# Converting double-precision weights on other engines, and keeping an activation in PSUM, in a convolution and MLP kernel

## The chip, the cores and the metric

The kernel runs on one core of a Trainium2 chip. The metric is the device time of one execution in microseconds (us). The core has five engines that run side by side and meet at semaphores: TensorE (PE in the profile, with its weight loads as PEld), VectorE (DVE), ScalarE (ACT), GpSimd (POOL) and SyncE (SP). SBUF is the working memory; PSUM holds the matmul results in eight banks.

## The reference

A sequence is filtered in the frequency domain, and the result goes through a two-layer MLP:

```python
X = np.fft.rfft(x, axis=1)                      # x: 8 x 3008 x 256, fp32
y = np.fft.irfft(X * (filt_r + 1j * filt_i), n=3008, axis=1).astype(np.float32)
h = y.reshape(24064, 256) @ w_in                # 256 x 2048
g = h * (1.0 / (1.0 + np.exp(-1.702 * h)))
out = (g @ w_out).astype(np.float32)            # 2048 x 256
```

[...]

## The kernel before, in words

Every fp32 product of the main part is made of three matmuls on a number split in two: a value rounded to the matmul type (suffix `h`, or `hi`) and the rest (suffix `l`, or `lo`); rounded by rounded, rounded by rest, rest by rounded.

The work has three parts. `first_fft` filters the first batch entry; its DMA-heavy part takes about the first 57 us. `weights` converts 16 units of weights (each 128 partitions x 512), interleaved with the end of `first_fft` and with the first MLP tiles. Then 48 MLP tiles of up to 512 tokens follow, 16 steps (`fc`) each, and the filtering of the next batch entry (`fft`, `signal`) is spread between the steps of the present one; the last batch entry's steps, from about 2150 us on, have nothing beside them.

One unit of weights (`weight`, lines 213 to 240): the upper and the lower 32 bits of each 64-bit number lie side by side as `top` and `low`. ACT takes |top| into `t` (L222); DVE clamps it (L227), shifts the exponent into place in `u` (L228), takes the bare exponent back into `t` (L229) and scales the low bits by it (L230); POOL adds the two (L231); ACT takes the absolute value (L232); DVE puts the sign back (L233). Then ACT rounds (`hi`, L238) and POOL takes the rest (`lo`, L239). The scratch tiles are the tile `w_tu` of the profile.

One MLP step (`mlp`, lines 526 to 566): `first(fc)` issues six matmuls (L539) into `ps`, a PSUM bank of tag `h`, of which there are two (`ps_h`, bufs=2). ACT reads the bank twice with the same activation: into `g` in SBUF as fp32 (L543), and into `gh` rounded (L544). DVE makes `gl = g - gh` (L545). `second(fc)` issues six matmuls (L555): four with `gh`, two with `gl`. `g`, `gh` and `gl` have two buffers each. The program text has `first(n+1)` ahead of `second(n)`.

The order of the instructions on each engine isn't that of the text: the framework's planner (`schedule_with_timeline_sim=True`) plays the program through with a model of the times and fixes an order for each engine; semaphores are set from the data that each instruction reads and writes. On the chip an engine takes its instructions in that fixed order. A PSUM bank may be written again when all its readers are done.

Of the kernel before, what the change touches and what calls it, by code (L numbers as in the profile page):

```python
# [9 lines left out]
F32 = mybir.dt.float32  # L10
F32R = mybir.dt.float32r
I64 = mybir.dt.int64
U32 = mybir.dt.uint32
AF = mybir.ActivationFunctionType
ALU = mybir.AluOpType
# [5 lines left out]
P = 128  # L21
# [4 lines left out]
LEAST = 2.0**-15  # L26
MOST = float(np.uint32(0x47EFFFFF).view(np.float32))
# [123 lines left out]
def tile_kernel(  # L151
# [9 lines left out]
    nc = tc.nc  # L161
    const = ctx.enter_context(tc.tile_pool(name="const", bufs=1))
    sb = ctx.enter_context(tc.tile_pool(name="sb", bufs=2))
# [49 lines left out]
    def weight(w, tu):  # L213

        if w.dtype != F32:
            rv = w.bitcast(U32).rearrange("p a (n k) -> p a n k", k=2)
            low, top = rv[:, :, :, 0], rv[:, :, :, 1]
            t, u = (a.bitcast(U32) for a in tu)
            w = t.bitcast(F32)


            ins = nc.scalar.activation(t.bitcast(F32), top.bitcast(F32), AF.Abs)  # L222
            if first[0]:
                tc.keep_in_program_order(ins)
                first[0] -= 1
            hi, lo = yield
            nc.vector.tensor_scalar(t.bitcast(F32), t.bitcast(F32), LEAST, MOST, ALU.max, ALU.min)  # L227
            nc.vector.tensor_scalar(u, t, 3, 0x40000000, ALU.logical_shift_left, ALU.bitwise_xor)  # L228
            nc.vector.tensor_scalar(t, u, 0xFF800000, None, ALU.bitwise_and)  # L229
            nc.vector.scalar_tensor_tensor(w, low, 2.0**-52, t.bitcast(F32), ALU.mult, ALU.mult)  # L230
            nc.gpsimd.tensor_tensor(w, u.bitcast(F32), w, ALU.add)  # L231
            nc.scalar.activation(w, w, AF.Abs)  # L232
            nc.vector.scalar_tensor_tensor(  # L233
                w.bitcast(U32), top, 0x80000000, w.bitcast(U32), ALU.bitwise_and, ALU.bitwise_or
            )
        else:
            hi, lo = yield
        nc.scalar.copy(hi, w)  # L238
        nc.gpsimd.tensor_tensor(lo, w, hi.bitcast(F32), ALU.subtract)  # L239
        yield  # L240

    def weights():

        todo, tus = [], None
        for i in range(NFC + 4):
            if i < NFC:
                todo.append(load_weight((w_out if i % 2 else w_in)[i // 2], f"w_{i}"))
            if i >= 4:
                if tus is None:
                    tus = const.tile([P, 4, 2, 2, D], F32, tag="zy", name="w_tu")  # L250
                for k in range(4 if i == 4 else 1):
                    k = k if i == 4 else i - 1
                    if k < NFC:
                        todo[k] = weight(todo[k], [tus[:, k % 4, m] for m in range(2)])
                        next(todo[k])
                n, o = divmod(i - 4, HALF)
                if n == len(wi_sb):
                    wi_sb.append(const.tile([P, 2, 2, DFF // 2], F32R, tag=f"wi_{n}", name=f"wi_{n}"))
                    wo_sb.append(const.tile([P, HALF, 2, D], F32R, tag=f"wo_{n}", name=f"wo_{n}"))
                if i % 2:  # L260
                    to = [wo_sb[n][:, o - 1 : o + 1, k] for k in range(2)]
                else:
                    to = [wi_sb[n][:, k, :, P * o : P * o + 2 * P] for k in range(2)]
                todo[i - 4].send(to)
            yield
# [260 lines left out]
    def mlp(b, t, y, nb, sums=(ps_o, "o")):  # L526

        w = P * nb
        pos, gs = [], {}

        def first(fc):
            ps = ps_h.tile([P, 512], F32, tag="h", name=f"h_{b}_{t}_{fc}")
            half, o = divmod(fc, HALF)
            c = slice(P * o, P * o + P)
            for n, (kc, wk, yk) in enumerate([(k, *q) for k in range(2) for q in ((0, 0), (0, 1), (1, 0))]):
                nc.tensor.matmul(ps[:, :w], wi_sb[half][:, wk, kc, c], y[:, yk, kc, :w], start=n == 0, stop=n == 5)  # L539
            g = sb.tile([P, 512], F32, tag="g", name=f"g_{b}_{t}_{fc}")  # L540
            gh = sb.tile([P, 512], F32R, tag="gh", name=f"gh_{b}_{t}_{fc}")
            gl = sb.tile([P, 512], F32R, tag="gl", name=f"gl_{b}_{t}_{fc}")
            nc.scalar.activation(g[:, :w], ps[:, :w], AF.Gelu_apprx_sigmoid)  # L543
            nc.scalar.activation(gh[:, :w], ps[:, :w], AF.Gelu_apprx_sigmoid)  # L544
            nc.vector.tensor_tensor(gl[:, :w], g[:, :w], gh[:, :w].bitcast(F32), ALU.subtract)  # L545
            gs[fc] = gh, gl

        def second(fc):
            if fc == 0:
                pos.extend(sums[0].tile([P, 512], F32, tag=sums[1], name=f"o_{b}_{t}_{m}") for m in range(2))  # L550
            gp = gs.pop(fc)
            wo = wo_sb[fc // HALF][:, fc % HALF]
            order = [(n, wk, gk, m) for n, (wk, gk) in enumerate(((0, 0), (1, 0), (0, 1))) for m in range(2)]
            for n, wk, gk, m in sorted(order, key=lambda q: q[3]) if fc == NFC - 1 else order:
                nc.tensor.matmul(  # L555
                    pos[m][:, :w], wo[:, wk, P * m : P * m + P], gp[gk][:, :w],
                    start=fc == 0 and n == 0, stop=fc == NFC - 1 and n == 2,
                )
            if fc == NFC - 1:
                o = sb.tile([P, 2, 512], F32, tag="out", name=f"out_{b}_{t}")  # L560
                nc.scalar.copy(o[:, 0, :w], pos[0][:, :w])
                nc.vector.tensor_copy(o[:, 1, :w], pos[1][:, :w])
                stores.append((out[:, :, done_w[0] : done_w[0] + w], o[:, :, :w]))
                done_w[0] += w

        return first, second

    def store():
# [40 lines left out]
    for n, (i, fc) in enumerate(turns):  # L609
        b, t = tiles[i]  # L610
# [61 lines left out]
```

## Time and profile before

| what | value |
|---|---|
| median of 3 runs | 2452.71 us (2450.07 to 2453.28) |
| time of the profiled execution | 2452.6 us |
| span of its instructions | 2450.6 us (2.0 us lie around it) |
| PE, DVE, ACT, POOL busy | 98%, 62%, 54%, 34% of the span |
| PE busy in the first 160 us | 125 us |
| PE idle after 160 us | 22 us |

The profile is one execution. A timeline row has a start, a duration, the engine, the line, the operation, what it writes and reads, and in square brackets the idle time of the engine before it with what ended it; a row may merge several instructions (xN). The other views group such rows.

### The profile page before, as it was taken

How to read it: one execution, taken by the hardware profiler on the slowest of the kernel's cores; microseconds unless marked ns; L12 is line 12 of the kernel's file. 1: busy time of each engine (PE TensorE's matmuls, PEld its weight loads, DVE VectorE, ACT ScalarE, POOL GpSimd, SP SyncE). 2: the span in 40 equal slices, each digit the busy share in tenths (PEclk: the TensorE clock that was granted, in tenths of full speed). 3: DMA queues.
4: the chain of work that ended last, by engine and by line, in shares of the span. 5: the costliest groups of instructions: out<-in, count | busy, mean ns of one | idle time of the engine just before them, and what ended most of it. 6: DMA issues, size and time to landing. Idle time of an engine off the chain costs nothing.

```text
span 2450.6 us, 31734 instructions
## 1 busy us (share of the span) xinstructions
PE 2394.2 (98%) x11082; PEld 1984.9 (81%) x11082; DVE 1531.4 (62%) x2167; ACT 1312.9 (54%) x2441; POOL 833.9 (34%) x714
## 2 busy tenths in 40 slices
PE   7799999999999999999999999999999999999999
PEld 6578888877888888888888887988888888898887
DVE  6966885488638883578636786368743777422322
ACT  5555655556555555555555565555555555444443
POOL 4743552265324441344323442234421444000000
PEclk9899999999999999999999999999999999999999
DMA  9234444545354435534344343444335443200000
GB/s 291 87 105 104 109 105 127 128 111 125 104 148 102 105 85 139 126 94 104 95 136 101 95 116 85 130 112 110 87 103 134 98 106 83 67 16 9 18 9 18
DMA packets 140927, 246.60 MB, mean 101 GB/s; under 512 B 15584, under 2 KB 81248, under 8 KB 140768
## 3 DMA queue, kind: packets, MB, share of 16 engines
q1 hardware_dynamic: 62528, 133.72, 19.4%
q10 hardware_dynamic: 53152, 66.80, 10.1%
q0 software_dynamic: 25088, 44.05, 9.3%
q8 instruction: 88, 1.44, 0.3%
q14 instruction: 71, 0.58, 0.1%
HBM read 150.67 MB, written 93.85 MB: 100 GB/s over the span
## 4 chain that ended last, share of the span: by engine, by line
PE 57%; DMA 2%; ACT 1%; issue 0%; ACTq 0%; SPq 0%; DVE 0%; POOLq 0%
PE o L555 26%; PE h L539 25%; PE i L512 2%; PE s L445 1%; PE i L445 1%; DMA b_d<-b 1%; DMA br<-b_d 1%; PE s L274 0%; PE s L273 0%; PE s L272 0%; DMA zy<-a_d 0%; DMA a_d<-al 0%; DMA x<-in_x_dram 0%; ACTq L419 0%; ACT g L543 0%
## 5 line engine op out<-in xcount | busy, mean ns | idle before, releaser
L539 PE MATMUL h<-y,wi 128*128 128x512 f32 (+1 forms) x4608 | 1172.5, 386 | 1.0 <-ACT y L520 1.0
L545 DVE TENSOR_TENSOR gl<-g,gh 128x512 fp32r<-128x512 f32 (+1 forms) x768 | 645.6, 843 | 751.9 <-ACT gh L544 677.6
L539 PEld LDWEIGHTS h<-y,wi 128*128 128x128 f32 x4608 | 861.9, 188 | 171.4 <-ACT y L520 1.4
L543 ACT ACTIVATE g<-h 128x512 f32<-128x512 f32 (+1 forms) x768 | 452.5, 589 | 909.6 <-PE h L539 767.1
L555 PE MATMUL o<-gh,wo 128*128 128x512 f32 (+1 forms) x3072 | 828.5, 389 | 6.6 <-ACT gh L544 6.1
L555 PEld LDWEIGHTS o<-gh,wo 128*128 128x128 f32 x3072 | 570.4, 188 | 125.0 <-ACT gh L544 11.4
L555 PE MATMUL o<-gl,wo 128*128 128x512 f32 (+1 forms) x1536 | 478.4, 388 | 14.3 <-DVE gl L545 14.1
L544 ACT ACTIVATE gh<-h 128x512 fp32r<-128x512 f32 (+1 forms) x768 | 448.9, 585 | 50.6 <-PE o L555 45.0
L460 POOL TENSOR_TENSOR zy<-c_buf,zy 48x512 fp32r<-48x512 f32 x224 | 335.3, 1497 | 93.6 <-DVE zy L459 83.6
L555 PEld LDWEIGHTS o<-gl,wo 128*128 128x128 f32 x1536 | 285.0, 188 | 76.2 <-DVE gl L545 22.2
L389 POOL TENSOR_TENSOR c_buf<-c_buf,u_buf 112x512 f32<-112x512 f32 x128 | 195.7, 1529 | 434.7 <-DVE c_buf L388 431.8
L409 POOL TENSOR_TENSOR xl<-x,xh 128x512 fp32r<-128x512 f32 x84 | 112.3, 1349 | 422.8 <-ACT xh L408 404.7
L428 POOL DMA_DIRECT2D zy<-a_d x224 | 128.3, 575 | 284.3 <-PE s L445 110.0
L396 DVE TENSOR_TENSOR c_buf<-s,c_buf 48x512 f32<-48x512 f32 x224 | 154.3, 689 | 14.9 <-ACT c_buf L395 8.6
L396 DVE TENSOR_TENSOR b<-i,b 48x512 f32<-48x512 f32 x224 | 154.1, 688 | 9.9 <-ACT b L395 3.8
L395 ACT COPY b<-i 48x512 f32<-48x512 f32 x224 | 130.1, 581 | 16.1 <-PE i L445 10.9
L395 ACT COPY c_buf<-s 48x512 f32<-48x512 f32 x224 | 130.2, 581 | 14.8 <-PE s L445 7.1
L459 DVE CAST zy<-c_buf 48x512 fp32r<-48x512 f32 x224 | 96.4, 430 | 52.2 <-POOL c_buf L389 48.5
L512 PEld LDWEIGHTS i<-tab,br 128*128 128x128 f32 x736 | 100.5, 194 | 19.1 <-issue 6.3
L512 PE MATMUL i<-tab,br 128*128 128x128 f32 x736 | 102.8, 279 | 7.8 <-DMA br<-b_d 4.4
L387 DVE TENSOR_TENSOR u_buf<-c_buf,f_buf 48x512 f32<-48x512 f32 x112 | 92.0, 821 | 3.6
L523 POOL CAST y<-carry 128x128 fp32r<-128x128 f32 x8 | 2.8, 377 | 262.4 <-PE h L539 262.3
(88 smaller groups left out, 1258.9 us busy)
## 6 DMA issues: line engine op xcount, KB each, us to landing
f_buf<-fs SPq DMA_DIRECT2D x224, 192.0 KB, 3.2
zy<-a_d POOLq DMA_DIRECT2D x224, 192.0 KB, 3.5
x<-in_x_dram SPq DMA_DIRECT2D x48, 512.0 KB, 4.8
out_dram<-out SPq DMA_DIRECT2D x44, 512.0 KB, 3.4
a_d<-ah ACTq DMA_DIRECT2D x84, 256.0 KB, 3.5
a_d<-al ACTq DMA_DIRECT2D x84, 256.0 KB, 3.8
b_d<-b ACTq DMA_DIRECT2D x112, 192.0 KB, 2.5
br<-b_d SPq DMA_DIRECT2D x84, 256.0 KB, 4.5
```

The lines of the kernel that those rows point to most:

```text
L389: nc.gpsimd.tensor_tensor(u1, u1, u2, ALU.add)
L395: nc.scalar.copy(dst[h], ps[k][o])
L396: nc.vector.tensor_tensor(dst[h], ps[k][h], dst[h], ALU.add)
L409: nc.gpsimd.tensor_tensor(xl, src, xh.bitcast(F32), ALU.subtract)
L428: nc.gpsimd.dma_start(zy[0][64 * k : 64 * k + 48, i % 2].rearrange("p k s d -> p k (s d)"), src.rearrange("n k s d -> n k (s d)"),)
L460: nc.gpsimd.tensor_tensor(y[o, k], u1[h], y[h, k].bitcast(F32), ALU.subtract)
L512: nc.tensor.matmul(ps[:, P * i : P * i + P], br[m][:, i], t2_sb, start=True, stop=True)
L539: nc.tensor.matmul(ps[:, :w], wi_sb[half][:, wk, kc, c], y[:, yk, kc, :w], start=n == 0, stop=n == 5)
L543: nc.scalar.activation(g[:, :w], ps[:, :w], AF.Gelu_apprx_sigmoid)
L544: nc.scalar.activation(gh[:, :w], ps[:, :w], AF.Gelu_apprx_sigmoid)
L545: nc.vector.tensor_tensor(gl[:, :w], g[:, :w], gh[:, :w].bitcast(F32), ALU.subtract)
L555: nc.tensor.matmul(pos[m][:, :w], wo[:, wk, P * m : P * m + P], gp[gk][:, :w], start=fc == 0 and n == 0, stop=fc == NFC - 1 and n == 2,)
```

## The change

Conversion: the two POOL instructions and the second absolute value on ACT go. The shifted number keeps its low 30 bits (a mask in place of the exclusive or), a new DVE instruction merges the two top bits of `top` into it, and so the sign is there from that point; the sum and the final rest are made on DVE. A unit then has two ACT and seven DVE instructions, where it had three ACT, five DVE and two POOL.

MLP step: `gh` is made first, and `g` is written over `h` in the PSUM bank; DVE subtracts from the bank. The tile `g` in SBUF goes, `gh` and `gl` get three buffers each.

```diff
@@ -224,19 +224,17 @@
             hi, lo = yield
-            nc.vector.tensor_scalar(t.bitcast(F32), t.bitcast(F32), LEAST, MOST, ALU.max, ALU.min)
-            nc.vector.tensor_scalar(u, t, 3, 0x40000000, ALU.logical_shift_left, ALU.bitwise_xor)
+            f = t.bitcast(F32)
+            nc.vector.tensor_scalar(f, f, LEAST, MOST, ALU.max, ALU.min)
+            nc.vector.tensor_scalar(u, t, 3, 0x3FFFFFFF, ALU.logical_shift_left, ALU.bitwise_and)
+            nc.vector.scalar_tensor_tensor(u, top, 0xC0000000, u, ALU.bitwise_and, ALU.bitwise_or)
             nc.vector.tensor_scalar(t, u, 0xFF800000, None, ALU.bitwise_and)
-            nc.vector.scalar_tensor_tensor(w, low, 2.0**-52, t.bitcast(F32), ALU.mult, ALU.mult)
-            nc.gpsimd.tensor_tensor(w, u.bitcast(F32), w, ALU.add)
-            nc.scalar.activation(w, w, AF.Abs)
-            nc.vector.scalar_tensor_tensor(
-                w.bitcast(U32), top, 0x80000000, w.bitcast(U32), ALU.bitwise_and, ALU.bitwise_or
-            )
+            nc.vector.scalar_tensor_tensor(w, low, 2.0**-52, f, ALU.mult, ALU.mult)
+            nc.vector.tensor_tensor(w, u.bitcast(F32), w, ALU.add)
         else:
             hi, lo = yield
         nc.scalar.copy(hi, w)
-        nc.gpsimd.tensor_tensor(lo, w, hi.bitcast(F32), ALU.subtract)
+        nc.vector.tensor_tensor(lo, w, hi.bitcast(F32), ALU.subtract)
@@ -537,12 +535,11 @@
-            g = sb.tile([P, 512], F32, tag="g", name=f"g_{b}_{t}_{fc}")
-            gh = sb.tile([P, 512], F32R, tag="gh", name=f"gh_{b}_{t}_{fc}")
-            gl = sb.tile([P, 512], F32R, tag="gl", name=f"gl_{b}_{t}_{fc}")
-            nc.scalar.activation(g[:, :w], ps[:, :w], AF.Gelu_apprx_sigmoid)
+            gh = sb.tile([P, 512], F32R, tag="gh", name=f"gh_{b}_{t}_{fc}", bufs=3)
+            gl = sb.tile([P, 512], F32R, tag="gl", name=f"gl_{b}_{t}_{fc}", bufs=3)
             nc.scalar.activation(gh[:, :w], ps[:, :w], AF.Gelu_apprx_sigmoid)
-            nc.vector.tensor_tensor(gl[:, :w], g[:, :w], gh[:, :w].bitcast(F32), ALU.subtract)
+            nc.scalar.activation(ps[:, :w], ps[:, :w], AF.Gelu_apprx_sigmoid)
+            nc.vector.tensor_tensor(gl[:, :w], ps[:, :w], gh[:, :w].bitcast(F32), ALU.subtract)
```

## Rows read from the trace of the kernel before

**Rows 1.** The page's first part: busy time, share, instructions of each engine

```profile
PE 2394.2 (98%) x11082; PEld 1984.9 (81%) x11082; DVE 1531.4 (62%) x2167; ACT 1312.9 (54%) x2441; POOL 833.9 (34%) x714
```

**Rows 2.** Busy time by stretch: length, engines, then granted clock, DMA share, GB/s

```profile
0.00:57.00 57.00, 46.95 (x298) 36.80 (x298) 38.39 (x57) 33.26 (x71) 22.15 (x23) 1.00 0.98 296
57.00:76.60 19.60, 9.48 (x42) 7.79 (x41) 15.77 (x23) 8.08 (x15) 17.23 (x10) 0.59 0.35 112
76.60:88.40 11.80, 8.95 (x36) 7.12 (x37) 11.69 (x21) 6.88 (x12) 6.06 (x5) 0.68 0.31 105
88.40:132.50 44.10, 34.39 (x138) 25.88 (x139) 43.59 (x50) 28.21 (x54) 30.46 (x22) 0.96 0.24 75
132.50:160.00 27.50, 25.63 (x110) 19.75 (x109) 18.88 (x23) 16.25 (x33) 18.23 (x12) 1.00 0.48 129
160.00:550.00 390.00, 382.03 (x1773) 315.89 (x1772) 269.86 (x374) 214.89 (x398) 161.71 (x137) 1.00 0.45 113
550.00:2450.60 1900.60, 1886.73 (x8691) 1571.69 (x8689) 1133.19 (x1623) 1005.28 (x1862) 578.05 (x510) 1.00 0.36 92
```

**Rows 3.** PE's waits from 57 to 160 us: waiter, releaser, total, times, longest

```profile
PE o L555 <- DVE gl L545: 10.6, 9, 4.1
PE i L366 <- POOL c_buf L389: 7.1, 3, 2.9
```

**Rows 4.** PE's waits after 160 us

```profile
PE o L555 <- ACT gh L544: 4.0, 9, 1.0
PE o L555 <- DVE gl L545: 3.5, 7, 0.9
```

**Rows 5.** Stretch 76.6 to 150, the conversion's scratch tile alone: DVE, ACT, POOL

```profile
76.60:150.00 73.40, 46.88 (x60) 21.99 (x35) 40.12 (x27) 0.92 0.29 89
```

**Rows 6.** DVE from 76.6 to 150 us by line and shape: count, busy, mean ns

```profile
L545 DVE TENSOR_TENSOR gl<-g,gh 128x512 fp32r<-128x512 f32 x16 | 20.0, 1247 | 1.2 <-ACT gh L544 1.2
...
L414 DVE TENSOR_TENSOR al<-s,ah 128x512 fp32r<-128x512 f32 x3 | 2.0, 679 | 0.0
```

**Rows 7.** DVE's timeline at 85 us, POOL without work there: start, duration

```profile
84.88 0.42 DVE L229 TENSOR_SCALAR w_tu<-w_tu 128x512 uint32<-128x512 uint32 x1
85.22 0.68 DVE L233 SCALAR_TENSOR_TENSOR w_tu<-w,w_tu 128x512 uint32<-128x512 uint32 x1
85.82 0.68 DVE L230 SCALAR_TENSOR_TENSOR w_tu<-w,w_tu 128x512 f32<-128x512 uint32 x1
```

**Rows 8.** POOL's timeline: one addition of the first filtering undisturbed, and its last

```profile
49.36 1.27 POOL L389 TENSOR_TENSOR c_buf<-c_buf,u_buf 112x512 f32<-112x512 f32 x1 [0.82 <-DVE c_buf L388]
...
63.67 3.78 POOL L389 TENSOR_TENSOR c_buf<-c_buf,u_buf 112x512 f32<-112x512 f32 x1 [1.12 <-DVE c_buf L388]
```

**Rows 9.** Timeline at 2200 us, MLP steps alone: one step followed through

```profile
2200.04 1.52 PE L539 MATMUL h<-y,wi 128*128 128x512 f32 x6
...
2202.09 0.59 ACT L544 ACTIVATE gh<-h 128x512 fp32r<-128x512 f32 x1
...
2202.72 0.69 DVE L545 TENSOR_TENSOR gl<-g,gh 128x512 fp32r<-128x512 f32 x1 [2.03 <-ACT gh L544]
...
2205.48 1.52 PE L539 MATMUL h<-y,wi 128*128 128x512 f32 x6
...
2206.84 0.62 PE L555 MATMUL o<-gl,wo 128*128 128x512 f32 x2
```

**Rows 10.** Timelines of PE and DVE at 310 us: two groups h, a subtraction

```profile
307.17 2.94 PE L539 MATMUL h<-y,wi 128*128 128x512 f32 x12
...
310.28 0.68 DVE L545 TENSOR_TENSOR gl<-g,gh 128x512 fp32r<-128x512 f32 x1
```

**Rows 11.** DVE's timeline: the first and last of 62 late subtractions after 160 us

```profile
231.50 2.38 DVE L545 TENSOR_TENSOR gl<-g,gh 128x512 fp32r<-128x512 f32 x2
...
2405.66 0.69 DVE L545 TENSOR_TENSOR gl<-g,gh 128x512 fp32r<-128x512 f32 x1
```

**Rows 12.** The whole execution by line and shape: the activation into `g`

```profile
L543 ACT ACTIVATE g<-h 128x512 f32<-128x512 f32 x704 | 421.0, 598 | 849.3 <-PE h L539 715.1 <-DVE gl L545 36.4 <-DVE b L396 35.0
```

## The prediction

> **What bounds the kernel now.** I read the busy times first [rows 1]: PE works 98% of the span and no other engine comes near, so nothing that the change takes from DVE, ACT or POOL counts unless it fills one of PE's gaps. All gaps together are 2450.6 - 2394.2 = 56.4 us, and the change adds no matmul and takes none away. So the question is where the gaps are. The stretches [rows 2] give it: from 57 to 160 us PE is busy 9.48 + 8.95 + 34.39 + 25.63 = 78.45 of 103 us, a gap of 24.6 us. Another 10 us lie before 57 us, where nothing of the change is on the path, and 22 us are spread over the 2290 us after 160 (8.0 up to 550 us, 13.9 behind it). The reader is to see two more things in those rows. From 76.6 to 132.5 us DVE is busy 55.3 of 55.9 us: there DVE is the bound, not PE. And from 57 to 88.4 us the granted clock is 0.59 and 0.68, so near the lower of TensorE's two levels (1.2 GHz), after stretches with PE often idle.
>
> Then the waits. From 57 to 160 us PE waits most for `gl` from DVE, 10.6 us in 9 waits, and for POOL's last additions of the first filtering, 7.1 us [rows 3]. After 160 us its waits for `gh` and `gl` are 4.0 and 3.5 us [rows 4].
>
> **Part A, the conversion and `gl` while DVE is the bound (76.6 to 150 us).** DVE is busy 46.88 us there with 60 instructions of the conversion, 12 units of five, 3.9 us a unit, while POOL spends 40.12 us on the same units [rows 5]. The 16 subtractions `gl` take 20.0 us at 1247 ns, while a subtraction of the same size whose first input is in PSUM takes 679 ns [rows 6]. With POOL idle, one-input instructions start 0.34 us apart and two-input ones 0.60 us apart [rows 7]. So more than half of DVE's time there is waiting inside the instruction beside POOL.
>
> After the change a unit is three one-input instructions and four two-input ones: 3 x 0.34 + 4 x 0.60 = 3.4 us, for 12 units 41 us, against 46.9. The two that come from POOL and the new merge weigh 1.8 us, the old merge goes with 0.6 us, and the waits beside POOL go with POOL's work. The 16 subtractions come to 16 x 0.60 = 9.6 us, against 20.0. DVE gets 5.9 + 10.4 = 16 us less. PE's gap from 76.6 to 160 us is 2.85 + 9.71 + 1.87 = 14.4 us, less than that, so PE is again the bound there and the gap is the limit. A DVE with some 55 of 73 us to do still answers late now and then, so I take 10 of the 14.4 us. Bounds: 0, if each `gl` still stands behind a burst of conversion, and 16, if the clock comes back earlier too. ACT loses one of three instructions per unit; ACT isn't the bound in any row of [rows 2], so that counts zero. The cover is ACT's idle time, 15.9 of 44.1 us in the third stretch.
>
> The subtraction now reads PSUM. The Trainium skill's page "VectorE: DVE Perf Modes", section "The TRN2 errata — SBUF-src ops pay a fixed extra latency per instruction", gives DVE 58 fixed cycles from SBUF but 120 from PSUM at 0.96 GHz, which speaks against the change: 65 ns more each, an estimate from that page, or 1 us over these 16, and part A would be 9. The trace decides otherwise: 679 ns with a PSUM input [rows 6] beside 0.69 us for `gl` from SBUF with POOL idle [rows 9].
>
> **Part B, the way to the first MLP step (57 to 76.6 us).** POOL's additions of the first filtering stay on POOL. Undisturbed one takes 1.27 us, the last one 3.78 us, behind a burst of DVE work [rows 8]. Four units are converted in that stretch, and four new merges (4 x 0.60 = 2.4 us) and four additions (2.4 us) now stand on DVE, in front of or among the last products. Who waits behind them is POOL's addition, then the inverse transform on PE. Cost 0 to 4.8 us. Against it, the old merges, rests and sums on POOL no longer hold up the copies and splits of the first tile's `y` on DVE: a gain of up to 4 us, by 11.69 of 11.8 us busy in the stretch after. I take +1, with -4 and +4.8 as ends.
>
> **Part C, the bank is held longer.** This is what the change adds: the six matmuls of `h(n+2)` write the bank of `h(n)`, and now wait for the subtraction, not for the second activation. Late in the kernel [rows 9] `gh` of the step that began at 2200.04 ends at 2202.68, its `gl` at 2203.41, and the next use of its bank starts at 2205.48: the slack falls from 2.8 to 2.07 us, and nothing waits. The matmuls with this `gl` come only at 2206.84, 1.36 us after the bank is used again: PE runs `h(n+2)` ahead of `gl(n)`, so a late `gl` has that much cover now, and loses it. PE's queue behind a late `gl` is everything.
>
> Where the filtering runs beside, DVE is late. At 310 us [rows 10] the second of the two groups starts at 308.53 (307.17 plus half of what two take), and the subtraction that reads its bank's former contents ends at 310.96: it would stall 2.4 us. I paired each `gl(n)` with `h(n+2)` through the timeline after 160 us: 62 are late, 55 us in sum, 36 of them before 550 us [rows 11], where DVE is busy 270 of 390 us [rows 2]. The sum overstates, since one stall moves all of PE's later work: the largest of each cluster (24 clusters) add up to 20 us, and to 14 when each `gl` takes 0.69 us. DVE's backlog is also smaller by the subtractions' waits beside POOL, and some of these places hold waits that are paid today. I take +6; ends 0 and 42 (all 62, with faster subtractions, none absorbed).
>
> **Part D, order and buffers.** `gh` is made first, so it comes one activation (0.5 us) earlier, and the third buffers free ACT and DVE from waiting for PE. That can take back the 4.0 + 3.5 us of [rows 4]: 0 to -7.5, I take -3.5.
>
> No row shows an activation that writes PSUM. The activation into SBUF takes 598 ns [rows 12]. Below, it could be a little faster; above, reading and writing the one bank in turn would at worst double it, 1.2 us, which takes the slack of 2.07 us to 1.5. I take 598 ns, the same engine on the same input. The Trainium skill's page "ScalarE: Activation LUTs", section "Step-by-step: what each stage is for", says that ScalarE writes PSUM faster than SBUF; no run here shows it, and the sum stays as it is.
>
> **Sum.** -10 + 1 + 6 - 3.5 = -6.5 us, against the profiled execution's 2452.6 us (its span 2450.6, 2.0 around it), which stands 0.1 us from the median of the runs: 2446.
>
> **Rivals.**
> 1. The bank decides: `h(n+2)` waits for `gl(n)` wherever the filtering crowds DVE. Speaks for it: the 62 late pairs, 36 within 390 us, and DVE at 270 of 390 us. Against: no late pair to speak of from 1000 us on except singles, and slack of 2 us in the plain steps. It decides once C passes 13 us: with C = +20 and A = -7, the sum is -7 + 1 + 20 - 3.5 = +10.5, 2463 us, slower. The page "PSUM — Partial Sum Buffer" of the Trainium skill, section "Summary: rules for kernel authors", asks to evacuate PSUM promptly; by that rule this rival would hold, and the trace so far shows the late pairs but no stall.
> 2. The conversion's gain is there but little arrives: DVE is no longer the bound, yet `gl` waits behind seven instructions of a unit, and four merges delay the start. A = -5, B = +3, C = +4, D = -2: 0, so 2453 us. For it: the four-unit burst ahead of the last addition [rows 8]. Against: DVE's 16 us.
> 3. The activation in place takes twice as long: ACT's 1312.9 us [rows 1] grow by some 450, still under PE, but `gl` comes 0.6 us later at each late pair: 62 x 0.6 = 37, of which by the ratio of C (14 of 55) some 9 us arrive: +3 on the sum, 2456 us.
>
> **Chances.** Forecast (2433 to 2447) 0.44, rival 1 0.25, rival 2 0.25, rival 3 0.06. Some 0.2% of the time (4.9 us) is about what a measurement can tell from no change. Rival 2 falls within it, and so does part of rival 3: faster 0.44, same 0.29, slower 0.27. Range: from A's full gap and D's full gain with B at 0 and C at 0 (-14.4 - 7.5 = -22, 2431) to rival 1 with B at its upper end (+14.3, 2467). The forecast's own range is 2433 to 2447.
>
> **What would show it.** A: from 76.6 to 150 us the unit's DVE time is near 3.4 to 3.9 us, `gl` near 0.68, POOL empty, and PE's wait for `gl` under 4 us. B: the first `h` group near 76.7 us. C: a wait of PE `h` for DVE `gl`, which is not in the rows of before, of some 6 us, mostly before 550 us. D: the waits for `gh` gone. An activation near 0.6 us. I am wrong if PE's idle time after 160 us grows past 35 us, or if the time before 160 us doesn't shrink.

## The result and the profile after

The changed kernel takes 2425.36 us (median; 2423.13 to 2428.3), the kernel before 2451.39 us beside it: ratio 0.9895, 95% interval 0.9878 to 0.9912, so 26 us faster. The prediction was 2446 us with a range from 2431: the sign was right, the time lies 5.6 us below the range. The profiled execution took 2425.99 us, its span is 2424.2 us.

The page's first part and the windows of the changed kernel, over the stretches of [rows 2] (columns as there):

```profile
PE 2388.0 (99%) x11082; PEld 1986.7 (82%) x11082; DVE 1400.1 (58%) x2199; ACT 1300.6 (54%) x2425; POOL 739.3 (30%) x682
```

```profile
0.00:57.00 57.00, 48.14 (x286) 37.52 (x286) 35.41 (x51) 31.87 (x68) 22.24 (x23) 0.94 0.98 281
57.00:76.60 19.60, 8.22 (x34) 6.49 (x35) 16.89 (x32) 3.17 (x7) 13.68 (x4) 0.62 0.54 186
76.60:88.40 11.80, 10.25 (x49) 8.76 (x49) 8.88 (x19) 6.97 (x13) 0.00 (x0) 0.61 0.06 23
88.40:132.50 44.10, 40.35 (x178) 31.65 (x177) 43.91 (x83) 29.94 (x56) 4.68 (x4) 1.00 0.29 90
132.50:160.00 27.50, 26.31 (x118) 20.69 (x117) 17.56 (x26) 16.36 (x31) 13.34 (x7) 1.00 0.58 160
160.00:550.00 390.00, 386.84 (x1813) 321.92 (x1812) 269.19 (x409) 224.61 (x416) 159.99 (x152) 1.00 0.50 120
550.00:2424.00 1874.00, 1867.88 (x8613) 1559.68 (x8611) 1008.28 (x1585) 987.69 (x1837) 525.36 (x492) 1.00 0.36 91
```

PE's idle time fell from 56.4 to 36.2 us, and its busy time for the same 11082 matmuls by another 6.2 us. After 160 us it stands idle 3.2 + 6.1 = 9.3 us, where it stood 22. DVE lost 131 us against [rows 1]; in the longest stretch, 550 us to the end, it lost 125, where no weight is converted.

To see where the 26 us arrive I followed both PE timelines and compared the times at which the same matmul work is done (each matmul weighed by its usual distance from one start to the next). At 31 us of the kernel before, the changed one is 2.9 us late; at 83 us 3.8 late; at 129 us 6.9 ahead; at 253 us 6.8; at 573 us 18.3; at 1485 us 21.7; at the end 26.4. So 19.6 of the 26.4 us come after 253 us. For the time after the conversion the prediction's parts C and D had added up to a loss of 2.5 us.

PE's waits of the changed kernel, first from 57 to 160 us, then after 160 us (waiter, releaser, total, times, longest):

```profile
PE i L364 <- POOL c_buf L387: 10.9, 3, 6.9
PE o L552 <- DVE gl L542: 3.0, 3, 1.2
```

```profile
PE o L552 <- DVE gl L542: 2.3, 7, 0.7
PE i L510 <- issue: 1.2, 1, 1.2
PE i L510 <- DMA br<-b_d: 0.5, 1, 0.5
```

Against [rows 3] the wait for `gl` went from 10.6 to 3.0 us, and that for POOL's additions grew from 7.1 to 10.9. After 160 us the wait for `gh` of [rows 4] is gone and that for `gl` is 2.3 us. There is no wait of PE `h` for `gl`, the one that the prediction priced.

The subtraction by shape after 160 us, of before and then of after (count, busy, mean ns):

```profile
L545 DVE TENSOR_TENSOR gl<-g,gh 128x512 fp32r<-128x512 f32 x685 | 579.6, 849 | 673.2 <-ACT gh L544 600.4 <-PE s L274 34.9 <-PE o L555 28.0
```

```profile
L542 DVE TENSOR_TENSOR gl<-h,gh 128x512 fp32r<-128x512 f32 x683 | 472.1, 691 | 814.8 <-ACT h L541 808.4 <-PE i L510 1.2
```

The reader is to see 849 ns beside 691: the same subtraction, 158 ns shorter on the mean, 107.5 us in all. It isn't an average of like with like. Two pairs of rows from the timelines show which ones shrink. Before, both inputs in SBUF, POOL at work:

```profile
191.01 1.29 POOL L409 TENSOR_TENSOR xl<-x,xh 128x512 fp32r<-128x512 f32 x1 [4.00 <-PE i L512]
191.17 1.69 DVE L545 TENSOR_TENSOR gl<-g,gh 128x512 fp32r<-128x512 f32 x1 [0.30 <-ACT gh L544]
```

After, one input in PSUM, POOL at work from 224.19 to 229.77:

```profile
224.19 5.58 POOL L458 TENSOR_TENSOR zy<-c_buf,zy 48x512 fp32r<-48x512 f32 x4
224.43 0.69 DVE L542 TENSOR_TENSOR gl<-h,gh 128x512 fp32r<-128x512 f32 x1
...
227.30 0.69 DVE L542 TENSOR_TENSOR gl<-h,gh 128x512 fp32r<-128x512 f32 x1
```

Before, the subtraction lasts until 192.86, 0.56 us past the end of POOL's instruction: it took 1.0 us more than the 0.69 us of [rows 9]. After, POOL's work doesn't touch it. A count over the whole traces after 160 us says the same. Of before's 685 subtractions 253 overlap an instruction with which POOL computes; they take 1117 ns on the mean and up to 1.84 us. The other 432 take 692 ns, and none over 0.70. In after 240 overlap such an instruction and take 691 ns, none over 0.70. POOL is freed as well: its additions of the later filtering take 1528 ns on the mean before and 1290 after.

The order on PE changed as well. One step late in the changed kernel's timeline:

```profile
2203.18 1.52 PE L537 MATMUL h<-y,wi 128*128 128x512 f32 x6
2204.54 1.07 PE L552 MATMUL o<-gh,wo 128*128 128x512 f32 x4
...
2205.44 0.62 PE L552 MATMUL o<-gl,wo 128*128 128x512 f32 x2
...
2205.90 1.52 PE L537 MATMUL h<-y,wi 128*128 128x512 f32 x6
2205.92 0.69 DVE L542 TENSOR_TENSOR gl<-h,gh 128x512 fp32r<-128x512 f32 x1 [3.83 <-ACT h L541]
```

In [rows 9] the next `h` group stood ahead of the `gl` matmuls. Now it stands behind them. In the instruction lists, `h(n+2)` precedes `gl(n)` in 752 of 766 steps before and in 21 after: the planner, which sees the bank held until `gl` is made, moved the matmul that can go first to the front.

### The profile page after: what moved, and what is told of

The parts are those of the page before. It is cut to its first block, busy times and chain, and to the rows that moved or that the text cites. A ratio compares the mean times of both kernels' runs of the same rounds, so it can differ in the third digit from the quotient of the medians.

```text
span 2424.2 us, 31325 instructions
## 1 busy us (share of the span) xinstructions
PE 2388.0 (99%) x11082; PEld 1986.7 (82%) x11082; DVE 1400.1 (58%) x2199; ACT 1300.6 (54%) x2425; POOL 739.3 (30%) x682
## 4 chain that ended last, share of the span: by engine, by line
PE 89%; DVE 6%; DMA 2%; issue 1%; ACT 1%; POOL 0%; SPq 0%; ACTq 0%; DVEq 0%; POOLq 0%
PE o L552 40%; PE h L537 40%; PE i L510 3%; PE i L443 2%; PE s L443 2%; DVE gl L542 1%; PE s L271 1%; PE s L272 1%; PE s L270 1%; DVE c_buf L394 1%; DVE u_buf L384 1%; DMA f_y<-in_filt_dram 1%; DMA f_o<-in_filt_dram 1%; DVE u_buf L385 0%; POOL c_buf L387 0%
## 5 line engine op out<-in xcount | busy, mean ns | idle before, releaser
L537 PE MATMUL h<-y,wi 128*128 128x512 f32 (+1 forms) x4608 | 1152.2, 385 | 0.2 <-ACT y L518 0.2
L542 DVE TENSOR_TENSOR gl<-h,gh 128x512 fp32r<-128x512 f32 (+1 forms) x768 | 522.0, 680 | 910.5 <-ACT h L541 903.8
L541 ACT ACTIVATE h<-h 128x512 f32<-128x512 f32 (+1 forms) x768 | 449.1, 585 | 0.0
L458 POOL TENSOR_TENSOR zy<-c_buf,zy 48x512 fp32r<-48x512 f32 x224 | 314.4, 1404 | 87.1 <-DVE zy L457 78.0
L552 PEld LDWEIGHTS o<-gl,wo 128*128 128x128 f32 x1536 | 283.8, 188 | 66.2 <-DVE gl L542 11.8
L387 POOL TENSOR_TENSOR c_buf<-c_buf,u_buf 112x512 f32<-112x512 f32 x128 | 174.0, 1360 | 424.7 <-DVE c_buf L386 419.3
L426 POOL DMA_DIRECT2D zy<-a_d x224 | 128.6, 576 | 347.6 <-PE s L443 188.8
L393 ACT COPY c_buf<-s 48x512 f32<-48x512 f32 x224 | 130.1, 581 | 11.8 <-PE s L443 4.1
L393 ACT COPY b<-i 48x512 f32<-48x512 f32 x224 | 130.1, 581 | 11.1 <-PE i L443 5.6
L457 DVE CAST zy<-c_buf 48x512 fp32r<-48x512 f32 x224 | 97.2, 434 | 29.5 <-POOL c_buf L387 25.1
L384 DVE SCALAR_TENSOR_TENSOR u_buf<-c_buf,f_buf 48x512 f32<-48x512 f32 x112 | 81.3, 726 | 3.6
```

Of the source, the lines that this page charges most:

```text
L387: nc.gpsimd.tensor_tensor(u1, u1, u2, ALU.add)
L393: nc.scalar.copy(dst[h], ps[k][o])
L426: nc.gpsimd.dma_start(zy[0][64 * k : 64 * k + 48, i % 2].rearrange("p k s d -> p k (s d)"), src.rearrange("n k s d -> n k (s d)"),)
L458: nc.gpsimd.tensor_tensor(y[o, k], u1[h], y[h, k].bitcast(F32), ALU.subtract)
L541: nc.scalar.activation(ps[:, :w], ps[:, :w], AF.Gelu_apprx_sigmoid)
L542: nc.vector.tensor_tensor(gl[:, :w], ps[:, :w], gh[:, :w].bitcast(F32), ALU.subtract)
```

## The experiments

Theory P: the gain after 250 us comes from the subtraction's input in PSUM, which frees it of POOL. Rivals: the new order of PE gives it (O), the longer hold costs or gives (H), the third buffers give it, the conversion gives it. All ratios are to the kernel before, run beside each. "From 253 us on" is the change against it by equal matmul work, as above; 19.6 us gained in the changed kernel.

| kernel | conversion | second activation | PE order | buffers | us | ratio (95%) | to 253 us | from 253 us on |
|---|---|---|---|---|---|---|---|---|
| after | new | bank | gl(n) first | 3 | 2425.36 | 0.9895 (0.9878 to 0.9912) | -6.8 | -19.6 |
| e1 | new | SBUF, g first | h(n+2) first | 2 | 2444.18 | 0.9956 (0.9943 to 0.9968) | -4.1 | -2.0 |
| e5 | old | bank | gl(n) first | 3 | 2432.15 | 0.9913 (0.9898 to 0.9929) | -1.5 | -19.1 |
| e2 | new | SBUF, gh first | h(n+2) first | 2 | 2449.7 | 0.9984 (0.9975 to 0.9993) | -11.2 | +8.9 |
| e9 | new | SBUF, gh first | gl(n) first | 2 | 2457.25 | 1.0015 (1.0005 to 1.0024) | -10.0 | +10.9 |
| e3 | new | SBUF, gh first, bank held | gl(n) first | 2 | 2462.46 | 1.0032 (1.002 to 1.0045) | -2.0 | +11.1 |
| e4 | new | bank | gl(n) first | 2 | 2429.92 | 0.99 (0.9887 to 0.9914) | -8.1 | -15.1 |
| e10 | new | bank | h(n+2) first | 3 | 2429.07 | 0.9904 (0.9887 to 0.9921) | -10.2 | -14.1 |
| e8 | new | as e1, little on POOL | h(n+2) first | 2 | 2424.14 | 0.9879 (0.9863 to 0.9896) | -15.3 | -13.1 |
| e11 | new | as e1, little on POOL | gl(n) first | 2 | 2414.6 | 0.9842 (0.9827 to 0.9856) | -9.0 | -28.2 |

**One part alone.** In e1 the MLP step of the kernel before, the activation into `g` first and two buffers each, stands beside the new conversion:

```diff
-            nc.scalar.activation(ps[:, :w], ps[:, :w], AF.Gelu_apprx_sigmoid)
-            nc.vector.tensor_tensor(gl[:, :w], ps[:, :w], gh[:, :w].bitcast(F32), ALU.subtract)
+            nc.scalar.activation(g[:, :w], ps[:, :w], AF.Gelu_apprx_sigmoid)
+            nc.vector.tensor_tensor(gl[:, :w], g[:, :w], gh[:, :w].bitcast(F32), ALU.subtract)
```

> The conversion of the changed kernel, the MLP step of the kernel before. Theory S (the two parts act in different places): the conversion acts before 200 us alone, where the changed kernel is 8 us ahead at equal matmul work; subtractions are still held beside POOL's other work, so some 4 to 8 us faster than before, 2443 to 2447 us, and after 200 us nothing changes (PE waits for gh and gl there 6 to 9 us in sum, as before). Rival T (freeing POOL and DVE early also clears the later stages): 15 us or more faster.

In e5 it is the other way round: the old conversion (POOL's two instructions, the absolute value and the old merge back, as on the minus side of the change's diff) with the new MLP step.

> The MLP step of the changed kernel, the conversion of the kernel before. Theory P (the bank held longer costs, the subtraction freed of POOL pays more): about 18 us faster than before after 200 us, and part of the startup gain too, since its subtractions no longer wait beside POOL: 2430 to 2436 us. Rival T (the two parts need each other, POOL must be free first): 2440 us or more.

e1 gains little after 253 us, and e5 gains 19.1 there, as much as the whole change. So the later gain is the MLP step's, but for those 2.0 us, and the conversion is worth what it does ahead of 253 us: 5.3 us between e5 and after. That figure is rough: it rests on one profile of each, e4 and e10 with after's conversion stand 8.1 and 10.2 us ahead there, and by the times the intervals of e5 and after overlap.

**Order of the activations.** e2 is e1 with the activation into `gh` ahead of the one into `g` (one line moved).

> The changed conversion, the rounded activation made first, but g in SBUF and two buffers each: one step more than conv_only. Theory P (port: the gain after 200 us comes from DVE no longer being held beside POOL in gl): within 2 us of conv_only, gl's mean stays near 840 ns. Rival G (gh is ready 0.5 us earlier): the 4 us of waits for gh after 160 us go, 4 to 6 us faster than conv_only. Rival O (order of gl and h on PE): no change, since the planner still puts h(n+2) ahead of gl(n) in 762 of 766 steps.

PE's wait for `gh` fell from 3.1 us in e1 to 0.8, but the kernel is 5.5 us slower than e1, which none of the expectations had. Some 9 us of its loss are one event near 1304 us: a wait of PE for a DMA of the filtering, 5.8 us long, and 6.8 us at a granted clock of 0.5, the lower of TensorE's two levels (1.2 GHz), behind it. The same event stands in e7, the other kernel below with these activations and this order (a wait of 6.0 us, near 1329 us), so it may belong to that plan and not to chance. Either way `gh` first, by itself, isn't the gain.

**The hold.** In e3 a copy of eight columns reads the bank of `h` after each subtraction, so that the bank is held as long as in the changed kernel; the planner then turns the order as there (16 of 766 steps left in the old one).

```diff
+            nc.vector.tensor_copy(seen[:, 0:8], ps[:, 0:8])
```

> As e2_gh_first, and after each gl a DVE copy of 8 columns out of the bank of h (some 0.1 us each), so that the bank is held until DVE is done as in the changed kernel, while g and gl still read SBUF. The planner then puts gl(n) ahead of h(n+2) in all but 16 steps, as for the changed kernel (21). Theory P (port): the wait for the bank is there without the relief, so slower than e2_gh_first by 6 to 20 us, by the late pairs of the trace of before. Rival O (the order by itself gives the gain): 12 to 18 us faster than e2_gh_first.

e3 is 12.8 us slower than e2, not faster; it has the hold and the order, and gains nothing from them. Its time is as theory P expected, the reason isn't: after 160 us PE waits 1.4 us for the bank, but 17.1 us for `gl`. And its copies cost DVE 122.5 us. e7 was to price those: the same copy out of `gl` in SBUF, with no hold.

```diff
+            nc.vector.tensor_copy(seen[:, 0:8], gl[:, 0:8].bitcast(F32))
```

> As e2_gh_first with the same 8-column DVE copy after each gl as in e3_hold, but out of gl in place of the bank: the copy's time without the hold; the planner leaves h(n+2) ahead of gl(n) in 758 steps. If the hold made e3_hold 12.8 us slower than e2_gh_first, this one is within 4 us of e2_gh_first's 2450; if DVE's extra 77 us did, it is near 2462.

It was no fair control (2471.83 us, ratio 1.0073, 1.0058 to 1.0088). The copies by line, e3's and then e7's:

```profile
L545 DVE COPY seen<-h 128x8 f32<-128x8 f32 x768 | 122.5, 160 | 5.2
```

```profile
L545 DVE COPY seen<-gl 128x8 f32<-128x8 f32 x768 | 272.6, 355 | 17.4
```

The same eight columns take 160 ns from PSUM and 355 ns from SBUF, a mean over 768; single ones last 1.16 us. Again it is POOL: after 160 us the 210 copies out of `gl` that overlap POOL's computing take 811 ns, the other 535 take 171; out of the bank it is 159 and 160 ns. So e7 has more of what it should have had equally, and it can't price e3.

**The operand.** e4 is the changed kernel with two buffers in place of three (`bufs=3` left out twice).

> The changed kernel with two buffers of gh and gl in place of three. Theory P (port): within 3 us of the changed kernel's 2425 us, since nothing of the port changes. Rival B (the third buffers let ACT and DVE run ahead): loses a good part of the 18 us gained after 200 us, 2433 us or more.

e9 is the control that e7 should have been: e2 with the new order and nothing else. An ordering edge, for which nothing waits on the chip, puts the first `h` matmul of step n+2 behind the last `gl` matmul of step n.

```diff
+                if n == 0 and len(lasts) > 1:
+                    tc.add_manual_dep(h.ins, lasts[-1], behind, reason="order")
```

> This kernel is e2_gh_first with one thing added: each step's h matmuls are planned behind the gl matmuls two steps before (the order in which the changed kernel and e3_hold stand), by an ordering edge that waits for nothing. No copy, no hold of the bank, no instruction more on VectorE. e2_gh_first took 2449.7 us, e3_hold 2462.5. Theory P (GpSimd's work holds VectorE's two-SBUF-input subtraction; the order alone gives nothing): no gain; gl stays near 0.84 us, and with 1.3 us less matmul work ahead of each gl the waits of PE for gl grow: 2450 to 2460. Rival O (the new order itself is where the changed kernel's gain of 20 us after 200 us comes from): about 2430, with PE's waits falling. Rival H (e3's loss of 13 us came from the order, not from the held bank and the copies): 2460 to 2465, as e3.

e9 and e4 have the same conversion, order of activations, order on PE and number of buffers. They differ in where the second activation is written, and with it in when the bank is free. First the subtraction's row after 160 us, of e9 and then of e4:

```profile
L545 DVE TENSOR_TENSOR gl<-g,gh 128x512 fp32r<-128x512 f32 x681 | 580.5, 853 | 711.2 <-ACT g L544 688.9 <-PE s L272 9.2 <-PE o L555 2.0
```

```profile
L542 DVE TENSOR_TENSOR gl<-h,gh 128x512 fp32r<-128x512 f32 x682 | 471.4, 691 | 813.7 <-ACT h L541 787.5 <-PE s L272 13.0 <-PE s L443 2.9
```

Then the largest sum of PE's waits there, of e9 and then of e4:

```profile
PE o L555 <- DVE gl L545: 13.8, 21, 1.7
```

```profile
PE o L552 <- DVE gl L542: 3.4, 8, 0.8
```

853 against 691 ns, waits of 13.8 against 3.4 us, and 1.0015 against 0.99 of the kernel before: 27 us by the medians, 26 us from 253 us on. So the operand alone brings a gain of that size, but the pair isn't a share of the 19.6 us: with the operand in SBUF the new order itself costs (e2 and e9, below). Against e1, the better kernel with the operand in SBUF, the gain from 253 us on is 12 us in the old order (e10) and 18 in the new one (after). The operand also acts in two ways that the runs don't separate: POOL is freed too. Its additions of the later filtering take 1449 ns in e9 and 1292 in e4, and PE's waits for POOL's `zy` are 3.0 and 0.8 us. The third buffers then bring 4.5 us by the profiles' second part (-15.1 to -19.6), which the ratios (0.99 and 0.9895) don't resolve. e4 lies between its two expected figures. e9 also prices e3: the held bank with all its copies costs 5 us more than the order alone by the medians, though the intervals overlap (1.0032, 1.002 to 1.0045, against 1.0015, 1.0005 to 1.0024). With 1.4 us of waits for the bank in e3, the hold itself is cheap.

**POOL taken away.** If POOL is what holds the subtraction, a kernel with the old MLP step and little work on POOL must gain as well. e8 is e1 with POOL's additions of the later filtering cut to eight of 256 columns (m). Both kinds of rests are left out: ACT makes plain copies in their place. So e8 and e11 leave out part of the filtering and show times only.

```diff
-        nc.gpsimd.tensor_tensor(u1, u1, u2, ALU.add)
+        nc.gpsimd.tensor_tensor(u1[:, :, 0:m], u1[:, :, 0:m], u2[:, :, 0:m], ALU.add)
-                nc.gpsimd.tensor_tensor(xl, src, xh.bitcast(F32), ALU.subtract)
+                nc.scalar.copy(xl, src)
-                nc.gpsimd.tensor_tensor(y[o, k], u1[h], y[h, k].bitcast(F32), ALU.subtract)
+                nc.scalar.copy(y[o, k], u1[h])
```

> As e1_conv_only, with POOL's arithmetic in the later filtering taken away: its additions are cut to 8 of 256 columns and the two kinds of rests are plain ACT copies (left out, so its output is not the reference's); POOL still issues its DMAs. g, gl and the order of PE stay as in e1. Theory P (port): gl's mean falls from 830 to about 690 ns with both inputs in SBUF, and the time falls to 2425 to 2435 us although ACT has some 180 us more to do. Rival H (the longer hold with its other order on PE is needed for the gain): gl's mean falls, but the time stays above 2440.

The subtraction after 160 us, both inputs in SBUF, and PE's waits:

```profile
L543 DVE TENSOR_TENSOR gl<-g,gh 128x512 fp32r<-128x512 f32 x680 | 469.4, 692 | 741.5 <-ACT gh L542 678.6 <-PE s L272 38.4 <-PE o L553 15.6
```

```profile
PE s L270 <- ACT xh L406: 7.6, 5, 2.4
PE s L440 <- DMA zy<-a_d: 2.3, 2, 1.5
```

692 ns, as with the PSUM input, and 2424.14 us against e1's 2444.18, in the old order and without the longer hold. The wait of PE's `o` for `gl`, 5.9 us in e1, isn't among its waits any more. Not all of the 20 us need be the subtraction: POOL's own results also come sooner, and ACT's later (the 7.6 us). By equal work only 11 of them come from 253 us on, and 7 were there at 57 us, ahead of what e8 alters (e1 is 10.0 us late there, e8 3.0). But the duration is settled: it is POOL's work that lengthens it, not the input's place as such.

**The order, with and without POOL's hold.** e11 is e8 with e9's edge; e10 is the changed kernel with the old order, made by an edge in the other direction (the `gl` matmuls of step n behind the last of the `h` matmuls of step n+2, `lasts[-1]`; 766 of 766 steps). In the last step of each tile e10 also issues the matmuls into `o` in the plain order, not one half of the output after the other. e10 is what the prediction took for granted.

```diff
+                if n == 2 and m == 0:
+                    tc.add_manual_dep(mm.ins, lasts[-1], behind, reason="order")
```

> This kernel is the changed one with the order of the kernel before on TensorE: the two gl matmuls of each step are planned behind the six h matmuls two steps later (766 of 766 steps). The bank is still held until gl is made. This is what the prediction assumed. Its step C: h(n+2) then waits for gl(n) at the 62 late pairs; 6 us more than the changed kernel (about 2431), ends 0 (2425) and 42 (2467), with a wait of PE h for DVE gl of about 6 us in the rows. Theory P says that VectorE is free of GpSimd here (gl 0.69 us), so that few of those pairs are late: 2425 to 2430. Rival O (the order gives the gain): about 2445, near the kernel before.

> This kernel is e8_no_pool (2424.1 us; GpSimd's additions of the later filtering cut to 8 of 256 columns, and the two kinds of rests made as ScalarE copies, so part of the filtering is left out) with the order edge of e9: h(n+2) planned behind gl(n). Theory P: with gl at 0.69 us the order is nearly free, 2422 to 2430. Rival H (the order costs by itself): 2434 or more. Rival O (the order gives): 2415 or less.

The one row in e10 for which the experiment was made, PE's wait for the bank after 160 us:

```profile
PE h L537 <- DVE gl L543: 0.7, 2, 0.6
```

e10 takes 2429.07 us, 0.9904 against 0.9895 for after: the new order is worth some 2 to 4 us by the times, 5.5 by equal work from 253 us on, and the intervals don't tell it from nothing. Between e8 and e11 the same turn brings 9.5 us, and there the intervals stand apart; between e2 and e9 it costs 7.5 us, apart as well. So the order costs where POOL holds `gl`: the `gl` matmuls lose the 1.36 us of `h` matmuls ahead of them, and PE's wait for `gl` goes from 6.6 us in e2 to 13.8 in e9. Where `gl` is on time the order may pay. e11 missed theory P's 2422 to 2430 us by 7 us and meets the figure that rival O had been given, 2415 or less. So rival O isn't out as a second cause beside the operand; what refutes it as the main one is e9, slower in the same order, and e10, which keeps all but 2 to 4 us in the old one. The edge in e11 also made the planner move matmuls of the filtering (the wait for `xh` of e8 isn't in e11), so its 9.5 us aren't the MLP order's alone.

**A version that beats both.** e6 takes up the one place where the change made things worse: POOL's last three additions of the first filtering go to DVE.

```diff
-            product(g, ps, c_buf[g % 3], f_s[g % 8])
+            product(g, ps, c_buf[g % 3], f_s[g % 8], nc.vector if g > 12 else nc.gpsimd)
...
-        nc.gpsimd.tensor_tensor(u1, u1, u2, ALU.add)
+        adds.tensor_tensor(u1, u1, u2, ALU.add)
```

> The changed kernel with the last three additions of the first filtering (entries 13 to 15) on DVE in place of POOL. In the changed kernel POOL's last addition lasts 7.79 us, the length of DVE's burst of merges, sums and shifts, and PE waits 6.9 us for it. Theory W (that starvation is what delays the first MLP step from 76.7 to 82.9 us): the wait of 6.9 us goes, the first h group starts near 76 us, and the kernel is 4 to 7 us faster than the changed one, 2418 to 2421 us. Rival D (DVE is the bound to 140 us, so an earlier start is given back): within 2 us of 2425.

2420.98 us, ratio 0.9864 (0.9849 to 0.9879), against after's 0.9895 (0.9878 to 0.9912): 4.4 us by the medians. PE's wait for the additions in the first 160 us:

```profile
PE i L364 <- DVE c_buf L387: 7.9, 3, 4.9
```

The wait went from 10.9 to 7.9 us, and the first `h` group starts at 80.30 us, not 82.89. The time is the expected one and the 3.0 us are there at the end by equal work (29.5 us ahead of the kernel before, after 26.4), but the wait didn't go, as had been expected, and the group doesn't start near 76 us. The two intervals touch.

## Why the prediction was right or wrong

**The step that failed.** The conversion came out near its price (parts A and B). What failed is the price of the new MLP step after 160 us: C put a wait of 6 us there that did not come, D let the step give back 7.5 us at most, and the sum had no term for a subtraction that POOL no longer holds. The runs showed 19.6 us gained from 253 us on, with the subtraction at 691 ns in place of 849.

**The bound and where to look.** PE was and is the bound. The prediction took 24.6 us of gaps between 57 and 160 us as the place and the 22 us after 160 as small change. It was the other way: 6.8 us came in ahead of 253 us, 19.6 behind. Of the two signs that would have spoken against it neither came: PE does 133.3 us of work in the first 160 us, not 125.4, and its idle time after 160 us shrank to 9.3.

**A, right in size, its working only in part.** Forecast -10. From 83 to 129 us the changed kernel gains 3.8 + 6.9 = 10.7 us; a little of it is a stretch at a granted clock of 0.5 that before has from 125.2 to 128.6 us and after hasn't. `gl` takes 680 ns there, POOL has no conversion, and the wait for `gl` is 3.0 us, under the 4 that were announced. The scratch tile's window, as [rows 5], with POOL no longer in it:

```profile
76.60:150.00 73.40, 50.51 (x88) 16.85 (x28) 0.94 0.33 97
```

88 instructions are 12.6 units of seven, 4.0 us a unit; the forecast said 3.4, the announced check up to 3.9. So the unit got no cheaper on DVE than the 3.9 us of before, and the 5.9 us that the working took from it did not come. The prediction's "more than half" of DVE's time spent waiting was too much by its own spacings, too: 12 x 2.2 + 9.6 = 36 of 66.9 us are work, so 46% is waiting. The 10 us on `gl` came, but they aren't the cause by themselves. In e5 `gl` takes 681 ns as well, beside the old conversion, and PE still waits for it and gains 2.7 us from 83 to 129; in e1, with the new conversion and `gl` from SBUF, the same stretch gains 14.2 us. e5's wait, from 57 to 160 us:

```profile
PE o L554 <- DVE gl L544: 8.0, 6, 3.1
```

So it takes the conversion without POOL, and that the size fits is in part luck. DVE is still busy 43.91 of 44.1 us from 88.4 to 132.5 us. It is full, but PE got its 40.35 us.

**B, right in size, though its announced check missed.** Forecast +1 with ends -4 and +4.8. POOL's last addition and PE behind it, from the changed kernel's timeline:

```profile
67.43 7.79 POOL L387 TENSOR_TENSOR c_buf<-c_buf,u_buf 112x512 f32<-112x512 f32 x1 [1.12 <-DVE c_buf L386]
...
75.28 0.95 PE L364 MATMUL i<-tab,c_buf 112*128 112x96 f32 x3 [6.89 <-POOL c_buf L387]
```

3.78 us became 7.79 and PE's wait behind it 2.88 became 6.89, 4.0 us more. POOL's addition ran beside an unbroken burst of the conversion on DVE, from 67.26 to 74.1 us, and came to its end only behind it. The first `h` group starts at 82.89, not near 76.7 as announced. Of these 6.2 us, 2.9 were late already at 31 us, behind a stretch at a granted clock of 0.5 (24.3 to 31.1 us) that e4 and e10 with the same conversion don't show; 4.0 are the addition's. But the addition's cost was given back, as the forecast's offset said. By equal work the changed kernel is 3.1 us late at 57 us, 7.8 at 70, 3.8 at 83 and 2.7 at 88.4; DVE, busy 11.69 of the 11.8 us from 76.6 us on before, is busy 8.88 of them. So B itself is +0.7 by 83 us. The 3 us at 31 us were in no term of the sum, which took the first 57 us as untouched.

**C, the step that failed.** Forecast +6: `h(n+2)` would wait for `gl(n)` at 62 late pairs. The changed kernel has no such wait. Two assumptions fell. The first was that PE's order stays as it was. It is made by a planner from the dependencies, and a changed dependency is a changed order; with `gl(n)` ahead of `h(n+2)`, a late `gl` is a wait of `o` for `gl` and never of `h`. The second weighs more. Even in the old order (e10) the wait is 0.7 us after 160 us. The late pairs were read from a trace in which the subtraction was itself held: the same pairing finds 58 pairs and 55 us in before, but 24 pairs and 11 us in e8, in the same order with little work on POOL. No run has the old order, the held bank and a subtraction that POOL still holds, so what C would have cost there stays open. (The start that the working reads as 308.53, half of 2.94 us after 307.17, is 308.64; nothing hangs on it.) The prediction had the mechanism in its hands: it read 1247 against 679 ns in [rows 6], wrote "waiting inside the instruction beside POOL", and used it in part A alone. After 160 us it only shortened C's list, from 20 to 14 us. It never asked what 158 ns in each of 685 subtractions, and up to 1.0 us where POOL is at work, cost PE today.

**D, the limit that was too low.** It capped the gain after 160 us at the two rows of [rows 4], 7.5 us. The gain is 19.6. Rows of waits are less than what stalls cost. A piece of PE's timeline in the kernel before shows it:

```profile
521.40 0.73 PE L555 MATMUL o<-gl,wo 128*128 128x512 f32 x2 [0.51 <-DVE gl L545]
...
528.64 0.73 PE L555 MATMUL o<-gl,wo 128*128 128x512 f32 x2 [0.58 <-DVE gl L545]
...
530.77 1.56 PE L555 MATMUL o<-gh,wo 128*128 128x512 f32 x4 [0.98 <-ACT gh L544]
532.13 2.76 PE L539 MATMUL h<-y,wi 128*128 128x512 f32 x6
```

Three waits, 2.07 us in all. Behind them four `gh` matmuls take 1.56 us, not 1.07, and six `h` matmuls 2.76, not 1.52 [rows 9]; the granted clock is 0.5 from 531.4 to 534.8 us. Around that place, from 516 to 573 us, the changed kernel gains 6.1 us, where all of before's waits from 510 to 580 us are 3.1 us; the slow matmuls add 1.7, and the rest isn't traced. It has no stretch at 0.5 between 85.7 us and its last instruction. PE's waits for DMAs fell too, to the 0.5 us shown above and 0.3. In the kernel before they were:

```profile
PE i L512 <- DMA br<-b_d: 4.4, 4, 1.6
...
PE s L442 <- DMA zy<-a_d: 1.2, 2, 0.7
```

The cap should have been all of PE's idle time after 160 us, 22 us, and what the clock lost behind it.

**The rivals.** Rival 1, the bank decides, is out: no wait of `h` in after, 0.7 us in e10. The Trainium skill's rule on evacuating PSUM promptly (page "PSUM — Partial Sum Buffer", section "Summary: rules for kernel authors"), cited beside it, would have kept the kernel from its largest gain; here the later release cost no wait in after and 0.7 us in e10. Rival 2 failed in its size, and rival 3 in its premise: the activation in place takes 585 ns over 768, the one into SBUF before 589. In after's view:

```profile
L541 ACT ACTIVATE h<-h 128x512 f32<-128x512 f32 (+1 forms) x768 | 449.1, 585 | 0.0
```

No rival stood on the side where the time came out: each asked what the change adds, none what it takes away from the 2290 us that looked well.

**What would have sized it.** The subtraction takes 849 ns in the kernel before and 853 in e9, with two SBUF inputs beside POOL's work; 691 with one input in PSUM, and 692 with two in SBUF where POOL has little to do (e8). The Trainium skill's page "SBUF — State Buffer", section "Who interferes with whom", states just that: a DVE instruction with two SBUF inputs contends with a GpSimd instruction that reads SBUF, one with at most one SBUF input doesn't, apart from some fast modes. The trace agrees: beside POOL's computing 1117 ns with two SBUF inputs, 691 with one. The prediction weighed 65 ns more for a PSUM input, an estimate from the Trainium skill's page "VectorE: DVE Perf Modes", section "The TRN2 errata — SBUF-src ops pay a fixed extra latency per instruction". They don't show, with 691 beside 692 ns.

**What stays open.** How much of the gain is the shorter subtraction and how much POOL's earlier results, in e4 and after as in e8; whether the order is worth the 2 to 4 us between e10 and after; and why the stretch at a granted clock of 0.5 at 24 us stands in some of these kernels and not in others.

## What to carry to other kernels

Where a two-input DVE instruction runs beside POOL's work, compare its mean in the crowded stretches with one that has an operand in PSUM; if they differ, count the difference over the whole kernel, not only where DVE is full. Don't cap what a change that removes stalls can gain at the wait rows: take all of the bound engine's idle time and the slower matmuls behind it. And where a planner orders the engines, a new dependency changes the order, so price the change under both orders.

## What was not expected of the hardware

- Being held goes both ways. An addition on POOL that takes 1.27 us alone [rows 8] took 7.79 beside a burst of DVE, across several DVE instructions, and ended 1.1 us behind the burst.
- An eight-column copy on DVE takes 160 ns from PSUM, but 355 ns on the mean from SBUF: 171 where POOL doesn't compute, 811 where it does.
- An activation that writes the PSUM bank it reads takes 585 ns, no longer than one into SBUF (589 ns).
- Waits of 0.5 to 1.0 us on PE, close together, were followed by 3.4 us at a granted clock of 0.5 at 531 us of the kernel before; the kernel after has none between 86 us and its end.
